# Cosine attention and GELU layer on one core: transposes earlier in the slot and in the row-sum bank, scores in twos, roots on ScalarE, preparation split over engines

## The chip, the cores and the metric

One core of a Trainium2 chip. The metric is the device time of one execution in microseconds (us), median of several; the profile is of one execution. Engines: PE (matmul), PEld (its weight loads), ACT (ScalarE), DVE (VectorE), POOL (GpSimd), SP (DMA issue). All runs named below count as fast (none is over 1.5% above the fastest of its kernel in the same session). The kernel before scatters: its fast runs lie between 735 and 747 us.

## The reference

Batch 8, 12 heads, 448 positions, head size 64; then a layer 768 to 2048 to 768.

```python
q_n = q / (norm(q) + 1e-6);  k_n = k / (norm(k) + 1e-6)
attn = softmax(q_n @ k_n.T / tau)          # tau = 0.1
x = (attn @ v), heads merged               # 3584 x 768
out = gelu_exact(x @ w_in) @ w_out
```

## The kernel before

The work goes in "pairs" of two heads, numbered g; a batch has six. A slot is one turn of the loop in `attention`. In the traces ACT, DVE, POOL and PE's matmuls run in the order in which the program gives their instructions (from 142.61 us of the kernel before DVE runs x, nq, se, rn and the copy, from 144.87 us POOL runs qkb, v, sq and sr); data and buffers add waits (POOL's qkb for rn 282.3 us in all, PE's `st` for an earlier Exp 12.6 us). The order of the calls is therefore the schedule: run 1 exchanges two calls, and the time changes by 84 us.

```python
def prep_square(g):
    nc.gpsimd.tensor_tensor(sq, qk_t[g], qk_t[g], ALU.mult)                 # POOL
    nc.vector.tensor_reduce(nq, sq, mybir.AxisListType.X, ALU.add)          # DVE
def prep_scale(g):
    nc.gpsimd.tensor_tensor(sr, nq, half, ALU.pow)                          # POOL: root
    nc.vector.tensor_scalar(se, sr, 1e-6, None, ALU.add)
    nc.vector.reciprocal(rn, se)
    for i in range(2):                                                      # q, then k
        nc.gpsimd.tensor_tensor(qkb[:, i]..., t[:, i], rn[:, i]..., ALU.mult)
def transposes(g):                       # 8 PE transposes into a bank of ps_mm
    ...
    nc.vector.tensor_copy(qkT, tp)
def scores(g, c):                        # chunk c: two matmuls, then Exp
    ...
def values(g, part):                     # part 0: o = pt*v, part 1: sm = pt*ones (row sums)
    ...
def normalise(g):
    nc.scalar.activation(ln, sm[:, :S], AF.Ln)
    nc.scalar.activation(rs, ln, AF.Exp, scale=-1.0)
    nc.vector.tensor_tensor(x_t[b][:, p, :], o[:, :S], rs, ALU.mult)

def attention(b, fill, first):           # fill: matmuls of the second dense layer ("fillers")
    for i in range(HP):
        ...
        scores(g, 0); run(u); scores(g, 1); run(u)
        if i > 0: values(g - 1, 0)
        scores(g, 2); run(u)
        if i > 0: values(g - 1, 1)
        scores(g, 3)
        if i > 0: normalise(g - 1)
        upkeep(g)                        # loads, prep_square(g+4), prep_scale(g+3)
        run(u)
        if i < HP - 1: transposes(g + 1)
        run(...)
```

After a batch's attention follows its first dense layer (16 groups of six matmuls and a Gelu). Its second layer is cut into single matmuls that fill PE's gaps in the next batch's attention. In the profiles `st` are the scores, `pt` their Exp, `hp` and `op` the products of the first and second dense layer; the "copy" is that of the transposed q and k (`qkT`), the "reduction" `nq`.

Of the kernel before, what the change touches and what calls it, by code (L numbers as in the profile page):

```python
# [8 lines left out]
F32 = mybir.dt.float32  # L9
BF16 = mybir.dt.bfloat16  # L10
AF = mybir.ActivationFunctionType
# [4 lines left out]
def kernel(  # L16
# [27 lines left out]

    consts = ctx.enter_context(tc.tile_pool(name="consts", bufs=1))
    wpool = ctx.enter_context(tc.tile_pool(name="wpool", bufs=1))
    qkp = ctx.enter_context(tc.tile_pool(name="qkp", bufs=4))
    sqp = ctx.enter_context(tc.tile_pool(name="sqp", bufs=2))
    vp = ctx.enter_context(tc.tile_pool(name="vp", bufs=8))
    nrm = ctx.enter_context(tc.tile_pool(name="nrm", bufs=3))  # L50
    qkbp = ctx.enter_context(tc.tile_pool(name="qkbp", bufs=3))
    qkTp = ctx.enter_context(tc.tile_pool(name="qkTp", bufs=3))
# [12 lines left out]
    make_identity(nc, ident)  # L65
    ones = consts.tile([CS, D], BF16)
    nc.vector.memset(ones, 1.0)
    half = consts.tile([CS, 2 * 2 * NC], F32)
    nc.vector.memset(half, 0.5)

    wi = wpool.tile([128, KD, d_ff], BF16, tag="wi")
    wo = wpool.tile([128, KF, d_model], BF16, tag="wo")
# [1 line left out]
    EXP_SET = "natural_log_exp_and_others"  # L74
    GELU_SET = "gelu_and_others"

    qk_t, v_t, sq_t, nq_t, qkb_t, qkT_t, pt_t, acc_t = {}, {}, {}, {}, {}, {}, {}, {}
    x_t, g_t = {}, {}


    def load_qk(g):
        b, p = divmod(g, HP)
        t = qkp.tile([CS, 2, 2, NC, D], F32, tag="qk", name=f"qk{g}")
        qk_t[g] = t
        for i, src in enumerate((q, k)):
            nc.sync.dma_start(
                out=t[:, i, :, :, :],
                in_=src[b, 2 * p:2 * p + 2].rearrange("h (p c) d -> p h (c d)", c=NC))

# [4 lines left out]
        nc.gpsimd.dma_start(  # L94
            out=t, in_=v[b, 2 * p:2 * p + 2].rearrange("h (p c) d -> p h (c d)", c=NC))

    def prep_square(g):
        sq = sqp.tile([CS, 2, 2, NC, D], F32, tag="sq", name=f"sq{g}")
        nc.gpsimd.tensor_tensor(sq, qk_t[g], qk_t[g], ALU.mult)  # L99
        nq = nrm.tile([CS, 2, 2, NC], F32, tag="nq", name=f"nq{g}")  # L100
        nc.vector.tensor_reduce(nq, sq, mybir.AxisListType.X, ALU.add)  # L101
        nq_t[g] = nq

    def prep_scale(g):
        nq = nq_t.pop(g)
        sr = nrm.tile([CS, 2, 2, NC], F32, tag="sr", name=f"sr{g}")
        nc.gpsimd.tensor_tensor(sr, nq, half, ALU.pow)  # L107
        se = nrm.tile([CS, 2, 2, NC], F32, tag="se", name=f"se{g}")
        nc.vector.tensor_scalar(se, sr, 1e-6, None, ALU.add)
        rn = nrm.tile([CS, 2, 2, NC], F32, tag="rn", name=f"rn{g}")  # L110
        nc.vector.reciprocal(rn, se)  # L111
        qkb = qkbp.tile([CS, 2, NC, 2, D], BF16, tag="qkb", name=f"qkb{g}")
        t = qk_t.pop(g)
        for i in range(2):
            nc.gpsimd.tensor_tensor(  # L115
                qkb[:, i].rearrange("p c h d -> p h c d"), t[:, i],
                rn[:, i].to_broadcast([CS, 2, NC, D]), ALU.mult)
        qkb_t[g] = qkb

    def transposes(g):  # L120
        qkb = qkb_t.pop(g)
        tp = ps_mm.tile([128, 2, NC, CS], BF16, tag="mm", name=f"tp{g}")
        for i in range(2):
            for c in range(NC):
                nc.tensor.transpose(tp[:, i, c, :], qkb[:, i, c].rearrange("p h d -> p (h d)"), ident)  # L125
        qkT = qkTp.tile([128, 2, NC, CS], BF16, tag="qkT", name=f"qkT{g}")
        nc.vector.tensor_copy(qkT, tp)  # L127
        qkT_t[g] = qkT


    def scores(g, c):
        qkT = qkT_t[g]
        st = ps_st.tile([CS, 2, 512], F32, tag="st", name=f"st{g}_{c}")
        for h in range(2):
            rows = slice(h * D, (h + 1) * D)
            nc.tensor.matmul(st[:, h, :S], lhsT=qkT[rows, 1, c, :], rhs=qkT[rows, 0, :, :],  # L136
                             start=True, stop=True)
        pt = ptp.tile([CS, 2, S], BF16, tag="pt", name=f"pt{g}_{c}")
        nc.scalar.activation(pt, st[:, :, :S], AF.Exp, scale=inv_tau)  # L139
        pt_t[g, c] = pt  # L140

    def values(g, part):
        if part == 0:
            acc_t[g] = (ps_acc.tile([128, 512], F32, tag="o", name=f"o{g}"),
                        ps_acc.tile([128, 512], F32, tag="sm", name=f"sm{g}"))
        dst = acc_t[g][part]
        for c in range(NC):
            for h in range(2):
                nc.tensor.matmul(dst[h * D:(h + 1) * D, :S],  # L149
                                 lhsT=v_t[g][:, h, c, :] if part == 0 else ones,  # L150
                                 rhs=pt_t[g, c][:, h, :], start=(c == 0), stop=(c == NC - 1))

    def normalise(g):
        b, p = divmod(g, HP)
        o, sm = acc_t.pop(g)
        ln = rcp.tile([128, S], F32, tag="ln", name=f"ln{g}")
        nc.scalar.activation(ln, sm[:, :S], AF.Ln)  # L157
        rs = rcp.tile([128, S], F32, tag="rs", name=f"rs{g}")
        nc.scalar.activation(rs, ln, AF.Exp, scale=-1.0)  # L159
        nc.vector.tensor_tensor(x_t[b][:, p, :], o[:, :S], rs, ALU.mult)  # L160
        v_t.pop(g)
        for c in range(NC):
            pt_t.pop((g, c))
# [29 lines left out]
    def load_wi(kd):  # L193
        nc.gpsimd.dma_start(out=wi[:, kd, :], in_=moe_w_in[kd * 128:(kd + 1) * 128, :])

    def load_wo(i):
        n = KF // 4
        nc.gpsimd.dma_start(
            out=wo[:, i * n:(i + 1) * n, :],
            in_=moe_w_out[i * n * 128:(i + 1) * n * 128, :].rearrange("(f p) d -> p f d", p=128))  # L200


    def attention(b, fill, first):
        fill = list(fill)
        per_slot = -(-len(fill) // HP)

        def run(n):
            for _ in range(min(n, len(fill))):
                fill.pop(0)()

        x_t[b] = xp.tile([128, HP, S], BF16, tag="x", name=f"x{b}")
        for i in range(HP):
            g = b * HP + i
            last_len = len(fill)
            u = per_slot // 5
            if not (i == 0 and not first):
                scores(g, 0)
                run(u)
                scores(g, 1)
            run(u)  # L220
            if i > 0:
                values(g - 1, 0)
            scores(g, 2)
            run(u)
            if i > 0:
                values(g - 1, 1)
            scores(g, 3)
            if i > 0:
                normalise(g - 1)
            upkeep(g)  # L230
            run(u)
            if i < HP - 1:
                transposes(g + 1)
            run(per_slot - (last_len - len(fill)) - (4 if len(fill) > 8 else 0))
        g = b * HP + HP - 1
        run(len(fill) - 20)
        values(g, 0)
        values(g, 1)
        normalise(g)
        run(len(fill))  # L240

    loaded = {"qk": 0, "v": 0, "sq": 0, "sc": 0}

    def upto(what, n, f):
        while loaded[what] < min(n, NG):
            f(loaded[what])
            loaded[what] += 1

    def upkeep(g):
        upto("qk", g + 6, load_qk)  # L250
        upto("v", g + 7, load_v)
        upto("sq", g + 5, prep_square)
        upto("sc", g + 4, prep_scale)


    nc.scalar.preload_act_table_set(EXP_SET)
    upto("qk", 4, load_qk)
    upto("v", 6, load_v)
    for n in range(1, 4):
        upto("sq", n, prep_square)  # L260
        upto("sc", n - 1, prep_scale)
    for kd in range(KD):
        load_wi(kd)
    for i in range(4):
        load_wo(i)
    upto("sc", 3, prep_scale)
    transposes(0)

    fill = []
    for b in range(B):  # L270
        attention(b, fill, b == 0)
        fill = []

        sb, hf = divmod(b, 2)
        if hf == 0:
            g_t[sb] = gp.tile([128, KF, 2 * S], BF16, tag="g", name=f"g{sb}")
        nc.scalar.preload_act_table_set(GELU_SET)
        for m in range(KF):
            hp = ps_mm.tile([128, 512], F32, tag="mm", name=f"hp{b}_{m}")
            for kd in range(KD):  # L280
                nc.tensor.matmul(hp[:, :S], lhsT=wi[:, kd, m * 128:(m + 1) * 128],  # L281
                                 rhs=x_t[b][:, kd, :], start=(kd == 0), stop=(kd == KD - 1))
            nc.scalar.activation(g_t[sb][:, m, hf * S:(hf + 1) * S], hp[:, :S], AF.Gelu)  # L283
            if m == KF - 3 and b + 1 < B:
                transposes((b + 1) * HP)
        if b + 1 < B:
            nc.scalar.preload_act_table_set(EXP_SET)  # L287
            scores((b + 1) * HP, 0)
            scores((b + 1) * HP, 1)
        for t in (range(3) if hf == 0 else range(3, 7)):  # L290
            fill += second_pieces(sb, t)
    for f in fill:
        f()

# [34 lines left out]
```

## Time and profile before

| | before |
|---|---|
| time, median of 4 fast runs | 744.1 us (736.4 to 745.0) |
| span of the profiled run | 734.4 us |
| busy: PE, ACT, POOL, DVE | 74%, 43%, 50%, 21% |
| first scores start | 37.1 us |
| first dense layer (batch 0) | 97.3 to 117.4 us |
| from there to the end of the last first layer, 7 periods | 591.5 us, 84.5 a period |
| rest | 25.5 us |
| granted PE clock | 0.904 |

The start until 117.4 us, the 7 periods and the rest add up to the span. No engine's share says what bounds the kernel.

### The profile page before, as it was taken

What the parts mean: (1) busy time and instruction counts of PE and PEld (TensorE: products, weight loads), DVE (VectorE), ACT (ScalarE), POOL (GpSimd) and SP (SyncE); (2) the same over time, 40 slices, a digit from 0 to 9 for tenths busy, and PEclk for the clock granted to TensorE, in tenths of its full rate; (3) what the DMA queues carried; (4) which work ended last, traced back from release to release, by engine and by line L of the source; (5) the groups of instructions that cost most, each with busy time, mean ns of one, the idle gap of its engine ahead of it and who ended that gap; (6) DMA issues with size and microseconds to landing.
All of it is one profiled execution on the core that took longest, in us unless ns stands there. A gap on an engine that the chain in (4) does not pass through costs nothing.

```text
span 734.4 us, 7898 instructions
## 1 busy us (share of the span) xinstructions
PE 545.8 (74%) x3200; PEld 249.3 (34%) x3200; DVE 156.3 (21%) x298; ACT 312.9 (43%) x432; POOL 367.2 (50%) x256
## 2 busy tenths in 40 slices
PE   0056588577968698757986879776987679867997
PEld 0022244223533244322542335322443235422454
DVE  1022211313121321231113231213212321121101
ACT  0044455444453345444453444543454444545430
POOL 8797754576256573466444762476644653330000
PEclk9999899879997999878998899887998889988999
DMA  7796210312202250032302323040502321000102
GB/s 156 153 222 126 62 33 7 78 38 54 77 12 54 79 122 17 14 97 59 79 8 54 84 55 77 6 110 8 130 7 54 82 55 48 0 23 1 43 4 84
DMA packets 42053, 45.35 MB, mean 62 GB/s; under 512 B 3360, under 2 KB 37664, under 8 KB 42016
## 3 DMA queue, kind: packets, MB, share of 16 engines
q1 hardware_dynamic: 27520, 33.04, 15.8%
q0 software_dynamic: 14496, 11.80, 10.8%
q8 instruction: 25, 0.41, 0.2%
q14 instruction: 12, 0.10, 0.0%
HBM read 45.61 MB, written 11.01 MB: 77 GB/s over the span
## 4 chain that ended last, share of the span: by engine, by line
PE 66%; DVE 12%; ACT 10%; issue 5%; POOL 4%; DMA 2%; SPq 0%; POOLq 0%
PE op L175 21%; PE hp L281 20%; PE st L136 10%; PE o L149 8%; PE sm L149 6%; DVE nq L101 4%; DVE x L160 3%; ACT rs L159 3%; ACT ln L157 3%; DVE qkT L127 3%; POOL sr L107 2%; ACT pt L139 1%; ACT L287 1%; DMA wi<-in_moe_w_in_dram 1%; ACT g L283 1%
## 5 line engine op out<-in xcount | busy, mean ns | idle before, releaser
L139 ACT ACTIVATE pt<-st 112x896 bf16<-112x896 f32 x192 | 173.4, 917 | 282.5 <-PE st L136 282.3
L115 POOL TENSOR_TENSOR qkb<-qk,rn 112x512 bf16<-112x512 f32 x96 | 98.1, 1043 | 284.5 <-DVE rn L111 282.3
L175 PE MATMUL op<-wo,g 128*128 128x384 bf16 x896 | 206.4, 365 | 0.2
L136 PE MATMUL st<-qkT 64*112 64x448 bf16 x384 | 88.8, 471 | 140.9 <-DVE qkT L127 128.1
L281 PE MATMUL hp<-x,wi 128*128 128x448 bf16 x768 | 148.1, 353 | 2.3 <-ACT g L283 1.7
L107 POOL TENSOR_TENSOR sr<-nq,half 112x16 f32<-112x16 f32 x48 | 140.2, 2920 | 0.0
L283 ACT ACTIVATE g<-hp 128x448 bf16<-128x448 f32 x128 | 69.7, 544 | 90.5 <-PE hp L281 90.5
L175 PEld LDWEIGHTS <-g 128*128 128x128 bf16 x896 | 78.3, 104 | 86.2 <-issue 56.9
L136 PEld LDWEIGHTS <-qkT 64*112 64x112 bf16 x384 | 27.3, 140 | 214.5 <-DVE qkT L127 140.3
L281 PEld LDWEIGHTS <-wi 128*128 128x128 bf16 x768 | 75.1, 98 | 72.4 <-issue 4.2
L99 POOL TENSOR_TENSOR sq<-qk 112x1024 f32<-112x1024 f32 x48 | 91.4, 1905 | 2.2 <-DMA qk<-in_k_dram 1.1
L160 DVE TENSOR_TENSOR x<-o,rs 128x448 bf16<-128x448 f32 x48 | 30.0, 625 | 243.8 <-ACT rs L159 243.8
L149 PE MATMUL o<-pt,v 112*64 112x448 bf16 x384 | 61.2, 454 | 13.5 <-DVE x L160 13.5
L127 DVE COPY qkT<-tp 128x896 bf16<-128x896 bf16 x48 | 28.3, 589 | 157.6 <-PE tp L125 157.6
L101 DVE TENSOR_REDUCE nq<-sq 112x16 f32<-112x1024 f32 x48 | 58.1, 1210 | 17.3 <-POOL sq L99 17.3
L179 DVE COPY ot<-op 128x384 f32<-128x384 f32 x56 | 30.7, 549 | 132.9 <-PE op L175 132.8
L125 PE MATMUL tp<-ident,qkb 112*128 112x112 bf16 x384 | 31.5, 234 | 27.1 <-POOL qkb L115 15.5
L149 PE MATMUL sm<-pt,ones 112*64 112x448 bf16 x384 | 49.4, 381 | 0.0
L149 PEld LDWEIGHTS <-v 112*64 112x64 bf16 x384 | 22.8, 131 | 48.5 <-issue 44.6
L125 PEld LDWEIGHTS <-qkb 112*128 112x128 bf16 x384 | 26.8, 109 | 36.2 <-POOL qkb L115 15.7
L94 POOL DMA_DIRECT2D v<-in_v_dram x48 | 35.6, 742 | 0.2 <-issue 0.2
L157 ACT ACTIVATE ln<-sm 128x448 f32<-128x448 f32 x48 | 25.8, 538 | 21.0 <-PE sm L149 21.0
(17 smaller groups left out, 96.1 us busy)
## 6 DMA issues: line engine op xcount, KB each, us to landing
qk<-in_q_dram SPq DMA_DIRECT2D x48, 224.0 KB, 4.0
qk<-in_k_dram SPq DMA_DIRECT2D x48, 224.0 KB, 4.4
v<-in_v_dram POOLq DMA_DIRECT2D x48, 112.0 KB, 3.1
wi<-in_moe_w_in_dram POOLq DMA_DIRECT2D x6, 512.0 KB, 11.1
wo<-in_moe_w_out_dram POOLq DMA_DIRECT2D x4, 768.0 KB, 24.9
out_dram<-ot SPq DMA_DIRECT2D x8, 336.0 KB, 3.1
out_dram<-ot SPq DMA_DIRECT2D x8, 288.0 KB, 3.0
out_dram<-ot SPq DMA_DIRECT2D x8, 240.0 KB, 2.9
```

What stands on the lines that cost most here:

```text
L99: nc.gpsimd.tensor_tensor(sq, qk_t[g], qk_t[g], ALU.mult)
L101: nc.vector.tensor_reduce(nq, sq, mybir.AxisListType.X, ALU.add)
L107: nc.gpsimd.tensor_tensor(sr, nq, half, ALU.pow)
L115: nc.gpsimd.tensor_tensor(qkb[:, i].rearrange("p c h d -> p h c d"), t[:, i], rn[:, i].to_broadcast([CS, 2, NC, D]), ALU.mult)
L125: nc.tensor.transpose(tp[:, i, c, :], qkb[:, i, c].rearrange("p h d -> p (h d)"), ident)
L136: nc.tensor.matmul(st[:, h, :S], lhsT=qkT[rows, 1, c, :], rhs=qkT[rows, 0, :, :], start=True, stop=True)
L139: nc.scalar.activation(pt, st[:, :, :S], AF.Exp, scale=inv_tau)
L149: nc.tensor.matmul(dst[h * D:(h + 1) * D, :S], lhsT=v_t[g][:, h, c, :] if part == 0 else ones, rhs=pt_t[g, c][:, h, :], start=(c == 0), st ...
L160: nc.vector.tensor_tensor(x_t[b][:, p, :], o[:, :S], rs, ALU.mult)
L175: nc.tensor.matmul(ps[:, :NH], lhsT=g_t[sb][:, kf, t * 128:(t + 1) * 128], rhs=wo[:, kf, ni * NH:(ni + 1) * NH], start=(kf == 0), stop=(kf ...
L281: nc.tensor.matmul(hp[:, :S], lhsT=wi[:, kd, m * 128:(m + 1) * 128], rhs=x_t[b][:, kd, :], start=(kd == 0), stop=(kd == KD - 1))
L283: nc.scalar.activation(g_t[sb][:, m, hf * S:(hf + 1) * S], hp[:, :S], AF.Gelu)
```

## The change

Its intent: keep PE from waiting at the turn of a slot, take work off POOL, and start sooner. The diff, cut to its core (buffer counts and the first pair's special cases left out):

```diff
-        nc.gpsimd.tensor_tensor(sr, nq, half, ALU.pow)
+    def root(g):
+        nc.scalar.activation(ln, nq, AF.Ln, bias=tiny)
+        nc.scalar.activation(sr, ln, AF.Exp, scale=0.5)
 ...
-        for i in range(2):
-            nc.gpsimd.tensor_tensor(
+        for i, eng in enumerate((nc.gpsimd, nc.vector)):
+            eng.tensor_tensor(
                 qkb[:, i]..., t[:, i], rn[:, i]..., ALU.mult)
 ...
-        tp = ps_mm.tile([128, 2, NC, CS], BF16, tag="mm", name=f"tp{g}")
+        tp = ps_acc.tile([128, 2, NC, CS], BF16, tag="sm", name=f"tp{g}")
 ...
+            upto("red", g + 3 if g else 2, reduce)
+            if g == 0 or i > 0:
+                scores(g, 0)                      # chunks 0 and 1
+            if i > 0:
+                run(share // 3)
+                upto("root", g + 3, root)
+                values(g - 1)                     # row sums first, then values
+                normalise(g - 1)
 ...
+            scores(g, 2)                          # chunks 2 and 3
+            if i < HP - 1:
+                transposes(g + 1)
 ...
+            upto("sc", g + 3, scale)
+            upto("sq", g + 4, square)
+            upto("qk", g + 8, load_qk)
+            upto("v", g + 4, load_v)
+            for _ in range(2 if b == 0 and i < 4 else 1):
+                if weights:
+                    weights.pop(0)()              # weight loads, one or two a slot
+            run(share - share // 3 if i else 6)
```

`upto(what, n, f)` calls `f` for every pair below n that has not had it: slot g takes the roots of pair g+2 and scales it, and squares pair g+3. `run(n)` gives n fillers. Besides, the first pair's preparation is spread over ACT, DVE and POOL, and the first two groups of a dense layer are interleaved.

More of the change, by code (lines that the diff above doesn't have):

```diff
@@ L46 @@
     wpool = ctx.enter_context(tc.tile_pool(name="wpool", bufs=1))
-    qkp = ctx.enter_context(tc.tile_pool(name="qkp", bufs=4))
+    qkp = ctx.enter_context(tc.tile_pool(name="qkp", bufs=5))
     sqp = ctx.enter_context(tc.tile_pool(name="sqp", bufs=2))
-    vp = ctx.enter_context(tc.tile_pool(name="vp", bufs=8))
+    vp = ctx.enter_context(tc.tile_pool(name="vp", bufs=6))
     nrm = ctx.enter_context(tc.tile_pool(name="nrm", bufs=3))
@@ L67 @@
     nc.vector.memset(ones, 1.0)
-    half = consts.tile([CS, 2 * 2 * NC], F32)
-    nc.vector.memset(half, 0.5)
+    tiny = consts.tile([CS, 1], F32)
+    nc.vector.memset(tiny, 1e-30)
     wi = wpool.tile([128, KD, d_ff], BF16, tag="wi")
@@ L75 @@
     GELU_SET = "gelu_and_others"
-    qk_t, v_t, sq_t, nq_t, qkb_t, qkT_t, pt_t, acc_t = {}, {}, {}, {}, {}, {}, {}, {}
+    qk_t, v_t, sq_t, nq_t, sr_t, qkb_t, qkT_t, pt_t, acc_t = {}, {}, {}, {}, {}, {}, {}, {}, {}
     x_t, g_t = {}, {}
@@ L85, in load_qk @@
         for i, src in enumerate((q, k)):
-            nc.sync.dma_start(
+            eng = nc.scalar if g == 0 and i == 1 else nc.sync
+            eng.dma_start(
                 out=t[:, i, :, :, :],
@@ L95, in load_v, with square, reduce, scale @@
             out=t, in_=v[b, 2 * p:2 * p + 2].rearrange("h (p c) d -> p h (c d)", c=NC))
-    def prep_square(g):
+    def square(g):
         sq = sqp.tile([CS, 2, 2, NC, D], F32, tag="sq", name=f"sq{g}")
-        nc.gpsimd.tensor_tensor(sq, qk_t[g], qk_t[g], ALU.mult)
-        nq = nrm.tile([CS, 2, 2, NC], F32, tag="nq", name=f"nq{g}")
-        nc.vector.tensor_reduce(nq, sq, mybir.AxisListType.X, ALU.add)
+        sq_t[g] = sq
+        t = qk_t[g]
+        if g == 0:
+            nc.scalar.activation(sq[:, 1], t[:, 1], AF.Square)
+            nc.vector.tensor_tensor(sq[:, 0], t[:, 0], t[:, 0], ALU.mult)
+        else:
+            nc.gpsimd.tensor_tensor(sq, t, t, ALU.mult)
+    def reduce(g):
+        sq = sq_t.pop(g)
+        nq = nrm.tile([CS, 2, 2, NC], F32, tag="nq", name=f"nq{g}")
+        if g == 0:
+            for i in range(2):
+                nc.vector.tensor_reduce(nq[:, i], sq[:, i], mybir.AxisListType.X, ALU.add)
+        else:
+            nc.vector.tensor_reduce(nq, sq, mybir.AxisListType.X, ALU.add)
         nq_t[g] = nq
-    def prep_scale(g):
+    def root(g):
         nq = nq_t.pop(g)
+        ln = nrm.tile([CS, 2, 2, NC], F32, tag="lq", name=f"lq{g}")
+        nc.scalar.activation(ln, nq, AF.Ln, bias=tiny)
         sr = nrm.tile([CS, 2, 2, NC], F32, tag="sr", name=f"sr{g}")
-        nc.gpsimd.tensor_tensor(sr, nq, half, ALU.pow)
+        nc.scalar.activation(sr, ln, AF.Exp, scale=0.5)
+        sr_t[g] = sr
+    def scale(g):
+        sr = sr_t.pop(g)
         se = nrm.tile([CS, 2, 2, NC], F32, tag="se", name=f"se{g}")
@@ L121, in transposes @@
         qkb = qkb_t.pop(g)
-        tp = ps_mm.tile([128, 2, NC, CS], BF16, tag="mm", name=f"tp{g}")
-        for i in range(2):
+        tp = ps_acc.tile([128, 2, NC, CS], BF16, tag="sm", name=f"tp{g}")
+        qkT = qkTp.tile([128, 2, NC, CS], BF16, tag="qkT", name=f"qkT{g}")
+        for i in (1, 0):
             for c in range(NC):
                 nc.tensor.transpose(tp[:, i, c, :], qkb[:, i, c].rearrange("p h d -> p (h d)"), ident)
-        qkT = qkTp.tile([128, 2, NC, CS], BF16, tag="qkT", name=f"qkT{g}")
@@ L127, in transposes, with scores @@
         nc.vector.tensor_copy(qkT, tp)
         qkT_t[g] = qkT
-    def scores(g, c):
+    def scores(g, c0):
         qkT = qkT_t[g]
-        st = ps_st.tile([CS, 2, 512], F32, tag="st", name=f"st{g}_{c}")
-        for h in range(2):
-            rows = slice(h * D, (h + 1) * D)
-            nc.tensor.matmul(st[:, h, :S], lhsT=qkT[rows, 1, c, :], rhs=qkT[rows, 0, :, :],
-                             start=True, stop=True)
-        pt = ptp.tile([CS, 2, S], BF16, tag="pt", name=f"pt{g}_{c}")
-        nc.scalar.activation(pt, st[:, :, :S], AF.Exp, scale=inv_tau)
-        pt_t[g, c] = pt
@@ L142, in values @@
-    def values(g, part):
-        if part == 0:
-            acc_t[g] = (ps_acc.tile([128, 512], F32, tag="o", name=f"o{g}"),
-                        ps_acc.tile([128, 512], F32, tag="sm", name=f"sm{g}"))
-        dst = acc_t[g][part]
-        for c in range(NC):
-            for h in range(2):
-                nc.tensor.matmul(dst[h * D:(h + 1) * D, :S],
-                                 lhsT=v_t[g][:, h, c, :] if part == 0 else ones,
-                                 rhs=pt_t[g, c][:, h, :], start=(c == 0), stop=(c == NC - 1))
+        for c in (c0, c0 + 1):
+            st = ps_st.tile([CS, 2, 512], F32, tag="st", name=f"st{g}_{c}")
+            for h in range(2):
+                rows = slice(h * D, (h + 1) * D)
+                nc.tensor.matmul(st[:, h, :S], lhsT=qkT[rows, 1, c, :], rhs=qkT[rows, 0, :, :],
+                                 start=True, stop=True)
+            pt = ptp.tile([CS, 2, S], BF16, tag="pt", name=f"pt{g}_{c}")
+            nc.scalar.activation(pt, st[:, :, :S], AF.Exp, scale=inv_tau)
+            pt_t[g, c] = pt
@@ new lines, in values @@
+    def values(g):
+        o = ps_acc.tile([128, 512], F32, tag="o", name=f"o{g}")
+        sm = ps_acc.tile([128, 512], F32, tag="sm", name=f"sm{g}")
+        acc_t[g] = (o, sm)
+        for dst in (sm, o):
+            for c in range(NC):
+                for h in range(2):
+                    nc.tensor.matmul(dst[h * D:(h + 1) * D, :S],
+                                     lhsT=ones if dst is sm else v_t[g][:, h, c, :],
+                                     rhs=pt_t[g, c][:, h, :], start=(c == 0), stop=(c == NC - 1))
@@ L200, in load_wo, with upto, attention @@
             in_=moe_w_out[i * n * 128:(i + 1) * n * 128, :].rearrange("(f p) d -> p f d", p=128))
-    def attention(b, fill, first):
+    weights = [lambda kd=kd: load_wi(kd) for kd in range(KD)] + [lambda i=i: load_wo(i) for i in range(4)]
+    done = {"qk": 0, "v": 0, "sq": 0, "red": 0, "root": 0, "sc": 0}
+    def upto(what, n, f):
+        while done[what] < min(n, NG):
+            f(done[what])
+            done[what] += 1
+    def attention(b, fill):
         fill = list(fill)
-        per_slot = -(-len(fill) // HP)
@@ L207, in run @@
         def run(n):
-            for _ in range(min(n, len(fill))):
+            for _ in range(max(0, min(n, len(fill)))):
                 fill.pop(0)()
         x_t[b] = xp.tile([128, HP, S], BF16, tag="x", name=f"x{b}")
+        tail = 20 if fill else 0
         for i in range(HP):
             g = b * HP + i
-            last_len = len(fill)
-            u = per_slot // 5
-            if not (i == 0 and not first):
+            share = (len(fill) - tail) // (HP - i) if i else 30
+            upto("red", g + 3 if g else 2, reduce)
+            if g == 0 or i > 0:
@@ L217, in attention @@
                 scores(g, 0)
-                run(u)
-                scores(g, 1)
-            run(u)
             if i > 0:
-                values(g - 1, 0)
-            scores(g, 2)
-            run(u)
-            if i > 0:
-                values(g - 1, 1)
-            scores(g, 3)
-            if i > 0:
-                normalise(g - 1)
-            upkeep(g)
-            run(u)
+                run(share // 3)
+                upto("root", g + 3, root)
+                values(g - 1)
+                normalise(g - 1)
+            else:
+                run(24)
+                upto("root", g + 3 if g else 2, root)
@@ L232, in attention @@
+            if g == 0:
+                upto("sc", 2, scale)
+            scores(g, 2)
             if i < HP - 1:
                 transposes(g + 1)
-            run(per_slot - (last_len - len(fill)) - (4 if len(fill) > 8 else 0))
+            if g == 0:
+                upto("sq", 3, square)
+                upto("red", 3, reduce)
+                upto("root", 3, root)
+            upto("sc", g + 3, scale)
+            upto("sq", g + 4, square)
+            upto("qk", g + 8, load_qk)
+            upto("v", g + 4, load_v)
@@ L235, in attention @@
+            for _ in range(2 if b == 0 and i < 4 else 1):
+                if weights:
+                    weights.pop(0)()
+            run(share - share // 3 if i else 6)
         g = b * HP + HP - 1
-        run(len(fill) - 20)
-        values(g, 0)
-        values(g, 1)
+        run(len(fill) - 8)
+        values(g)
         normalise(g)
         run(len(fill))
-    loaded = {"qk": 0, "v": 0, "sq": 0, "sc": 0}
-    def upto(what, n, f):
-        while loaded[what] < min(n, NG):
-            f(loaded[what])
-            loaded[what] += 1
@@ L249, in upkeep @@
-    def upkeep(g):
-        upto("qk", g + 6, load_qk)
-        upto("v", g + 7, load_v)
-        upto("sq", g + 5, prep_square)
-        upto("sc", g + 4, prep_scale)
-    nc.scalar.preload_act_table_set(EXP_SET)
-    upto("qk", 4, load_qk)
-    upto("v", 6, load_v)
-    for n in range(1, 4):
-        upto("sq", n, prep_square)
-        upto("sc", n - 1, prep_scale)
-    for kd in range(KD):
-        load_wi(kd)
-    for i in range(4):
-        load_wo(i)
-    upto("sc", 3, prep_scale)
-    transposes(0)
@@ L269, with first @@
-    fill = []
-    for b in range(B):
-        attention(b, fill, b == 0)
-        fill = []
+    def first(b):
         sb, hf = divmod(b, 2)
@@ L277, with mm, gelu @@
         nc.scalar.preload_act_table_set(GELU_SET)
-        for m in range(KF):
-            hp = ps_mm.tile([128, 512], F32, tag="mm", name=f"hp{b}_{m}")
-            for kd in range(KD):
-                nc.tensor.matmul(hp[:, :S], lhsT=wi[:, kd, m * 128:(m + 1) * 128],
-                                 rhs=x_t[b][:, kd, :], start=(kd == 0), stop=(kd == KD - 1))
-            nc.scalar.activation(g_t[sb][:, m, hf * S:(hf + 1) * S], hp[:, :S], AF.Gelu)
-            if m == KF - 3 and b + 1 < B:
-                transposes((b + 1) * HP)
+        hps = {}
+        def mm(m, kds):
+            for kd in kds:
+                nc.tensor.matmul(hps[m][:, :S], lhsT=wi[:, kd, m * 128:(m + 1) * 128],
+                                 rhs=x_t[b][:, kd, :], start=(kd == 0), stop=(kd == KD - 1))
+        def gelu(m):
+            nc.scalar.activation(g_t[sb][:, m, hf * S:(hf + 1) * S], hps.pop(m)[:, :S], AF.Gelu)
+        for m in range(KF):
+            if m == KF - 5 and b + 1 < B:
+                transposes((b + 1) * HP)
+            if m != 1:
+                hps[m] = ps_mm.tile([128, 512], F32, tag="mm", name=f"hp{b}_{m}")
+            if m == 0:
+                hps[1] = ps_mm.tile([128, 512], F32, tag="mm", name=f"hp{b}_1")
+                mm(0, range(KD - 1))
+                mm(1, range(KD - 1))
+                mm(0, (KD - 1,))
+            else:
+                mm(m, (KD - 1,) if m == 1 else range(KD))
+            gelu(m)
         if b + 1 < B:
@@ L288 @@
             scores((b + 1) * HP, 0)
-            scores((b + 1) * HP, 1)
-        for t in (range(3) if hf == 0 else range(3, 7)):
-            fill += second_pieces(sb, t)
+    upto("qk", 1, load_qk)
+    nc.scalar.preload_act_table_set(EXP_SET)
+    upto("qk", 5, load_qk)
+    upto("v", 3, load_v)
+    upto("sq", 1, square)
+    upto("red", 1, reduce)
+    upto("sq", 2, square)
+    upto("root", 1, root)
+    upto("sc", 1, scale)
+    transposes(0)
+    fill = []
+    for b in range(B):
+        attention(b, fill)
+        first(b)
+        sb, hf = divmod(b, 2)
+        fill = [f for t in (range(3) if hf == 0 else range(3, 7)) for f in second_pieces(sb, t)]
     for f in fill:
```

## The prediction

The ring's sum came to 8.05 us: the steps that stand add up to 6.98, and two terms are cut, one for the root's two instructions (with it the sum was 7.5) and one for a longer time of POOL's half beside DVE's. Both are also in H+11.9, in the four rounds of 32.2 us, in the 26.8, 59 and 63.8 us of the start and in the totals 68.3, 69, 82 and 590.5.

The 0.7 us for cold stretches is derived from no trace. "Cold" is a low granted PE clock, such as the 0.56 at 145.2 to 148.4 us of the kernel before and the 0.50 at 156.8 to 160 us; "warm" is 1.00.

> **What bounds the kernel now.** I first read the busy table by stage, because a share over the whole span mixes an attention stage with a dense matmul stage. The columns are the stretch, its length, busy time of PE, PEld, DVE, ACT and POOL, the granted PE clock, DMA share and GB/s.
>
> ```profile
> 37.00:99.25 62.25, 36.28 (x190) 14.49 (x190) 16.37 (x31) 28.03 (x37) 49.96 (x35) 0.92 0.59 121
> 118.00:183.20 65.20, 46.73 (x277) 19.62 (x276) 16.18 (x31) 30.43 (x38) 40.00 (x29) 0.84 0.22 50
> 183.20:202.80 19.60, 19.36 (x110) 9.93 (x108) 2.64 (x5) 8.72 (x17) 5.08 (x3) 1.00 0.29 74
> ```
>
> Attention of one batch takes 65.2 us (even batches 66.6), the first dense layer 19.6 us. In the dense layer PE is busy throughout at clock 1.00; the change cannot shorten that. In attention no engine fills the stretch: PE 46.7 of 65.2 at a clock of only 0.84, ACT 30, POOL 40. So it is bound by a chain of waits. The chain that ended last, read over one slot (a head pair) of that stretch, shows which:
>
> ```profile
> 141.43 0.55 ACT ln L157
> ...
> 142.00 0.58 ACT rs L159
> ...
> 142.61 0.62 DVE x L160
> 143.24 1.12 DVE nq L101
> ...
> 144.73 0.49 DVE qkT L127
> ...
> 145.26 0.40 PE st L136 x2
> ...
> 151.77 0.79 issue
> ```
>
> The same ln comes again at 152.56: the slot is 11.1 us. Up to 145.26 PE stands (scores of the next pair need qkT, and its copy stands on DVE behind x and the reduction nq). Then PE works through scores, fillers (L175), values and row sums until 151.73; the 0.79 us is the rest of the last Exp; then ln, rs, x again. So about 4.3 us of PE idle a slot are in the loop, and the 6.5 us of PE work are slow besides: by stretches, the clock was 0.56 at 145.2 to 148.4 and 0.92 at 148.4 to 152.5. POOL is not in this loop, although it is the busiest after PE there:
>
> ```profile
> L107 POOL TENSOR_TENSOR sr<-nq,half 112x16 f32<-112x16 f32 x48 | 140.2, 2920 | 0.0
> ...
> L99 POOL TENSOR_TENSOR sq<-qk 112x1024 f32<-112x1024 f32 x48 | 91.4, 1905 | 2.2 <-DMA qk<-in_k_dram 1.1
> ```
>
> The third thing is the start, read in the timeline:
>
> ```profile
> 23.26 3.32 POOL L194 DMA_DIRECT2D wi<-in_moe_w_in_dram  x6
> ...
> 33.16 2.93 POOL L107 TENSOR_TENSOR sr<-nq,half 112x16 f32<-112x16 f32 x1
> ...
> 37.11 0.99 PE L136 MATMUL st<-qkT 64*112 64x448 bf16 x4 [20.51 <-DVE qkT L127]
> ```
>
> The first scores wait until 37.1 us although the transposes of pair 0 were done at 16.6: the copy stands on DVE behind the scaling of pair 2, whose root stood on POOL behind ten weight issues, two of which waited 3.6 us for earlier weights to land.
>
> [...]
>
> **The change part by part.**
> Removed: 48 POOL roots of 2.92 us (140 us busy), and one of the two POOL scalings of a pair (1.04). POOL busy time falls from 7.7 us a pair (2.92 + 2×1.04 + 1.91 + 0.74, the last for issuing v) to 1.04+1.91+0.74 = 3.7. None of that was in the slot's loop, only in the start. [...]
>
> PE order: fillers, row sums, values, scores of chunks 2 and 3, then the transposes of the next pair in the row-sum bank, then more fillers. Scores of the next pair no longer wait for ln, rs, x and nq in a row. Work per slot at the warm rates of the chain: scores 0.8, sums 0.88, values 0.88, transposes 0.56, fillers 0.165 each; 9 fillers in odd batches (96, less 30 in slot 0 and 20 at the end, over 5) make 4.6 us, 15.6 in even ones 5.7. [...] If nothing else waited a slot would take 5.5 to 6 us.
>
> But the order of the built program makes a new loop, through POOL. Root(g+3) on ACT stands ahead of ln(g). It needs the reduction of sq(g+3); sq(g+3) stands on POOL behind the Q scaling of pair g+2; that needs rn(g+2), which on DVE stands behind x(g-1) and the copy qkT(g+1); and x needs ln(g-1), which stands on ACT behind root(g+2). Once round is one slot:
> [...] ln 0.57; rs 0.61; x 0.54; copy 0.48; se 0.20; rn until POOL starts 0.39; Q scaling 0.99; sq 1.95; reduction 1.25. The durations are start-to-start steps of the trace before[...]. Sum 7.5 us. The K half reaches DVE about 0.1 us before the Q half reaches POOL (0.14 us from rn's end to POOL's start in the trace)[...].
> PE then idles (8.05 less 4.6 to 5.7) 2.4 to 3.4 us a slot[...].
>
> A batch, from the end H of the dense layer before: the last Gelu, a table load of 1.28 and two Exp go beside 24 fillers (4 us); scores, transposes and copy until H+6.0; then se, rn, POOL, reduction, root: H+11.9. Four rounds: +32.2. Then ln and rs 1.2, two Exp 1.75, sums and values 1.85, eight fillers 1.3: 50.1 us. Dense layer 18.2. In all 68.3 us where the kernel before needs 85.3 (84.5 and 86.2 alternating). For cold stretches I add 0.7: 69.
>
> Start: pair 1 lands at 8.5 us, as now; POOL squares it (1.9), scales Q of pair 0 (1.0); transposes, copy, first scores at 12.6 us instead of 37.1. Pairs 1 and 2 ramp up one after the other (root, scaling, square, reduction each), root(3) about 26.8, four rounds to 59, then 2.95 and 1.85 to 63.8, dense layer to 82; before it ended at 117.4. Weights: the software queue's 10.8% of the span are 79 us of all 16 DMA engines for 11.8 MB, so 6.3 MB of weights need 42 us, spread over slots 0 to 5; with 13 pairs of q, k (1.6 us each) and 10 of v (0.8) about 71 us, just in time for the second layer at 82.
> End: 25.5 us from the last dense layer's end, unchanged.
> Sum: 82 + 7×69 + 25.5 = 590.5 us span. Timed runs before lie between 736.4 and 744 for a span of 734.4, so I add little: 592.
>
> **Rivals.**
> (a) The loop through POOL is looser than I think, and PE and ACT bound the slot at about 6 us: 36 to 40 rounds less 2 us, about 515. For it: POOL is busy only 3.7 us a slot. Against: the order of the instructions, which is fixed.
> [...]
> (c) PE drops to half clock in every slot and becomes the bound with 15.6 fillers[...]: slots of 8.5 to 9.5, about 625.
> (d) The weights, now spread, land late or hold POOL's queue in the first batch: 5 to 15 us more. For it: weight pieces took 11 to 25 us to land. Against: the sum above.
>
> **Range and chances.** The stretches that the change touches lose 35 us at the start and 7×16.3 later; even rival (c) with (d) stays near 640. Rounds of 7 to 9 us give 550 to 634; I take 545 to 632. Faster by over 2% is as good as certain (98 in 100); the rest is for a fault I overlooked.
>
> **What would show it right or wrong.** Right: in the chain, slots of about 8 us in which Q scaling, sq (POOL), nq (DVE), Ln, Exp, ln, rs (ACT), x and the copy follow each other, with PE hardly in it outside the dense layer; the same slot in odd and even batches; POOL idle only ahead of qkb, put down to rn; one of POOL's qkb and DVE's new one longer than alone, or started late; first scores near 12.6 us. Wrong: slots near 6 us with PE on the chain (a), slots that grow with the fillers and a clock below 0.7 (c), waits of hp or op for DMA (d), a first dense layer that ends far from 82.

## The result, and the profile after

| | before | after | predicted |
|---|---|---|---|
| time, median of 4 fast runs | 744.1 us | 584.2 us (583.9 to 585.6) | 592 (545 to 632) |
| span of the profiled run | 734.4 | 582.6 | 590.5 |
| first scores start | 37.1 | 11.6 | 12.6 |
| end of first dense layer | 117.4 | 82.8 | 82 |
| seven periods | 591.5 | 474.3 | 483 |
| rest | 25.5 | 25.5 | 25.5 |
| POOL busy | 367 | 196 | |
| PE busy, clock | 546, 0.904 | 492, 0.945 | |

The ratio is 0.787 (95% interval 0.782 to 0.793). Ratios are the mean time of one kernel's fast runs over that of the other's in the same rounds, so not quite the ratio of the medians. The profiled execution of the kernel before took 736.2 us, less than the median; so the spans differ by less than the medians do. All outputs are right.

Of the span's 151.8 us, 34.6 came from the start and 117.2 from the seven periods. The busy table by stage (stretch, length, busy time and count of PE, PEld, DVE, ACT, POOL, clock, DMA share, GB/s) for the kernel after, attention of batch 1 and its dense layer:

```profile
83.30:131.60 48.30, 38.75 (x277) 19.13 (x278) 21.19 (x39) 31.63 (x51) 22.63 (x17) 0.93 0.33 78
131.60:150.80 19.20, 18.76 (x107) 9.69 (x106) 2.31 (x3) 8.38 (x17) 0.97 (x2) 1.00 0.19 47
```

Attention went from 65.2 to 48.3 us; still no engine fills it, and POOL is now busy for less than half of it, where it was busy for 40 of 65 us. The shares of the chain that ended last, by engine, for the kernel after:

```profile
PE 49%; POOL 20%; DVE 16%; ACT 9%; issue 4%; DMA 1%; POOLq 0%; SPq 0%
```

POOL was 4% of the chain at 367 us of work and is 20% at 196. The chain over one slot (start, length, what) shows how:

```profile
105.37 1.45 POOL qkb L135
106.82 1.86 POOL sq L106
...
108.70 1.23 DVE nq L115
...
109.96 0.32 ACT lq L121
...
110.30 0.22 ACT sr L123
110.51 0.44 ACT ln L178
...
111.00 0.57 PE tp L146 x8
...
111.59 0.63 DVE x L181
112.21 0.53 DVE qkT L147
...
113.29 1.45 POOL qkb L135
```

This is the ring that the prediction wrote down: Q scaling, square, reduction, root, normalising, copy, and the next Q scaling 7.92 us later. PE is in it with the eight transposes only, which wait for ln, because they write the bank that it reads, and end at the same moment as rs (111.6 us). The rounds repeat at 7.9 us in odd and even batches alike. The two halves of the scaling, in the groups of the kernel after (busy time, mean ns of one, idle time before them):

```profile
L135 POOL TENSOR_TENSOR qkb<-qk,rn 112x512 bf16<-112x512 f32 x48 | 70.3, 1464 | 324.4 <-DVE rn L131 284.7
...
L135 DVE TENSOR_TENSOR qkb<-qk,rn 112x512 bf16<-112x512 f32 x48 | 34.1, 710 | 1.8 <-DVE rn L131 0.2
```

POOL's half has the same shape as before, when it took 1043 ns. Now it takes 1464.

### The profile page after: what moved, and what is told of

Same layout as the page of the kernel before. It is cut to its first block, busy times and chain, and to the rows that moved or that the text cites. A ratio compares the mean times of both kernels' runs of the same rounds, so it can differ in the third digit from the quotient of the medians.

```text
span 582.6 us, 7930 instructions
## 1 busy us (share of the span) xinstructions
PE 492.1 (84%) x3200; PEld 248.1 (43%) x3200; DVE 195.6 (34%) x348; ACT 324.7 (56%) x529; POOL 196.3 (34%) x159
## 4 chain that ended last, share of the span: by engine, by line
PE 49%; POOL 20%; DVE 16%; ACT 9%; issue 4%; DMA 1%; POOLq 0%; SPq 0%
PE hp L289 25%; PE op L196 15%; POOL sq L106 12%; POOL qkb L135 9%; DVE nq L115 7%; DVE qkT L147 3%; DVE x L181 3%; PE tp L146 3%; ACT ln L178 3%; PE st L157 2%; ACT lq L121 2%; PE o L170 2%; ACT rs L180 2%; PE sm L170 2%; DVE rn L131 2%
## 5 line engine op out<-in xcount | busy, mean ns | idle before, releaser
L160 ACT ACTIVATE pt<-st 112x896 bf16<-112x896 f32 x192 | 164.9, 910 | 34.0 <-PE st L157 33.4
L135 POOL TENSOR_TENSOR qkb<-qk,rn 112x512 bf16<-112x512 f32 x48 | 70.3, 1464 | 324.4 <-DVE rn L131 284.7
L196 PE MATMUL op<-wo,g 128*128 128x384 bf16 x896 | 175.6, 346 | 0.0
L196 PEld LDWEIGHTS <-g 128*128 128x128 bf16 x896 | 85.2, 102 | 70.8 <-issue 28.2
L146 PE MATMUL tp<-ident,qkb 112*128 112x112 bf16 x384 | 30.1, 226 | 69.3 <-ACT ln L178 58.2
L157 PE MATMUL st<-qkT 64*112 64x448 bf16 x384 | 65.7, 413 | 9.1 <-DVE qkT L147 8.0
L121 ACT ACTIVATE lq<-nq,tiny 112x16 f32<-112x16 f32 x48 | 14.8, 308 | 96.8 <-DVE nq L115 95.7
L170 PE MATMUL o<-pt,v 112*64 112x448 bf16 x384 | 48.7, 379 | 0.0
L157 PEld LDWEIGHTS <-qkT 64*112 64x112 bf16 x384 | 22.2, 136 | 49.9 <-issue 28.0
L135 DVE TENSOR_TENSOR qkb<-qk,rn 112x512 bf16<-112x512 f32 x48 | 34.1, 710 | 1.8 <-DVE rn L131 0.2
L170 PEld LDWEIGHTS <-ones 112*64 112x64 bf16 x384 | 19.8, 118 | 32.8 <-issue 27.0
```

What stands on the lines that cost most here:

```text
L135: eng.tensor_tensor(qkb[:, i].rearrange("p c h d -> p h c d"), t[:, i], rn[:, i].to_broadcast([CS, 2, NC, D]), ALU.mult)
L146: nc.tensor.transpose(tp[:, i, c, :], qkb[:, i, c].rearrange("p h d -> p (h d)"), ident)
L157: nc.tensor.matmul(st[:, h, :S], lhsT=qkT[rows, 1, c, :], rhs=qkT[rows, 0, :, :], start=True, stop=True)
L160: nc.scalar.activation(pt, st[:, :, :S], AF.Exp, scale=inv_tau)
L170: nc.tensor.matmul(dst[h * D:(h + 1) * D, :S], lhsT=ones if dst is sm else v_t[g][:, h, c, :], rhs=pt_t[g, c][:, h, :], start=(c == 0), st ...
L196: nc.tensor.matmul(ps[:, :NH], lhsT=g_t[sb][:, kf, t * 128:(t + 1) * 128], rhs=wo[:, kf, ni * NH:(ni + 1) * NH], start=(kf == 0), stop=(kf ...
```

## The experiments

The theory to be tested: the kernel after is bound by the ring of 7.92 us, not by any engine's work; the kernel before by ln, rs, x, nq and the copy in a row ahead of the next scores. The main rival: PE, cold in places (clock 0.60 from 113.3 to 116.3 us of the kernel after) and 84% busy, sets the time, and the gain came from work taken off POOL.

**1. The square first.** Only the order of two calls:

```diff
-            upto("sc", g + 3, scale)
-            upto("sq", g + 4, square)
+            upto("sq", g + 4, square)
+            upto("sc", g + 3, scale)
```

> Edit: in the changed kernel the square of pair g+3 is given to POOL ahead of the scaling of pair g+2, nothing else. Theory (the slot of 7.92 us is the ring root, ln, rs, x, copy, se, rn, Q scaling, square, reduction, root; the square is in it only because it stands behind the Q scaling on POOL): the square is done in POOL's idle time, the ring is cut at rn, and a slot falls to what comes next, about 5.9 us (ACT 5.1, PE 4.6 to 5.7, and a shorter ring through the K half and the reduction on DVE, about 5.2). Five rounds a batch less 2 us: about 500 us, 485 to 520. Rival (PE, cold between bursts, sets the slot, and POOL's place on the chain is only an effect): within 2% of 584.

Measured: 499.9 us (497.9 to 500.7), 0.678 of the kernel before. The slots are 5.0 to 5.5 us in odd batches and 5.1 to 5.9 in even ones, which have more fillers; PE is 94% busy at a clock of 0.995, and the chain by engine reads:

```profile
PE 78%; DVE 10%; ACT 7%; issue 2%; DMA 1%; POOL 1%; SPq 0%; POOLq 0%
```

POOL fell from 20% of the chain to 1% with the same instructions. The rival falls. What bounds this kernel is, by its chain, PE for the most part, and in the first slots of odd batches the shorter ring through the K half (5.05 us a round).

**2. The K half later.** The scaling is cut into two calls; DVE's comes after the next reduction:

```diff
             upto("red", g + 3 if g else 2, reduce)
+            if g:
+                upto("sk", g + 2, scale_k)       # K half, on DVE
 ...
-            upto("qk", g + 8, load_qk)
+            upto("qk", g + 7, load_qk)
```

> Edit: the K half of the scaling on DVE is given one slot later, after the next reduction, so that it no longer runs beside POOL's Q half (q and k are loaded one pair less ahead, so that their buffers suffice). Theory ([...] POOL's Q half takes 1.46 us instead of 1.04 because of that): POOL's qkb has a mean of 1.02 to 1.06 us, the slot falls from 7.92 to about 7.45 us, 38 rounds: 567 us, 560 to 575. Rival (POOL's qkb is longer for another reason, or the wait moves to the transposes): qkb stays above 1.3 us or the time within 5 us of 584.

Measured: 567.6 us (566.6 to 568.0). POOL's half in the groups of this run:

```profile
L138 POOL TENSOR_TENSOR qkb<-qk,rn 112x512 bf16<-112x512 f32 x48 | 50.9, 1060 | 327.6 <-DVE rn L131 232.2 <-PE st L164 46.4 <-DMA out_dram<-ot 25.9
```

Apart from DVE's half it takes 1060 ns again, and the Q scalings follow each other at 7.48 us. So the overlap with DVE costs POOL 0.4 us a pair, and 17 us in all.

**3 and 4. The same additional work on POOL, inside and outside the ring.** One more multiplication of a pair, result unused, at one of two places:

```diff
             upto("sc", g + 3, scale)
+            if done["sq"] < min(g + 4, NG):      # run 3: between scaling and square
+                more(done["sq"])
             upto("sq", g + 4, square)
             ...
             upto("v", g + 4, load_v)
+            if g + 3 < NG:                       # run 4: after the square and the v issue
+                more(g + 3)
```

> Edit: one more multiplication of POOL of 1.9 us a pair, its result unused, put between the Q scaling and the square, in the ring. Theory: each of some 38 rounds is 1.87 us longer: 584 + 71 = 655 us, 645 to 665; slots of 9.8 us. Rival (POOL has 4 us of idle time a slot and is not the bound): under 595.

> Edit: the same additional multiplication of 1.9 us a pair, put behind the square and the v issue, where POOL waits for the next rn. Theory: POOL's busy time grows by the same 90 us as in the run before, but outside the ring: within 6 us of 584, slots stay at 7.9 us. Rival (the sum of POOL's work counts[...]): 600 to 655.

Measured: 653.5 us (652.5 to 660.9) inside, 584.5 us (583.8 to 585.6) outside. POOL's busy time is the same in both (280 and 282 us, against 196). Inside, the rounds are 9.78 us; outside, 7.92. POOL's busy time bounds nothing; its place in the order does.

**5. The root by POOL's power again,** in the place in which Ln and Exp stood:

```diff
-        nc.scalar.activation(ln, nq, AF.Ln, bias=tiny)
-        nc.scalar.activation(sr, ln, AF.Exp, scale=0.5)
+        nc.gpsimd.tensor_tensor(sr, nq, half, ALU.pow)
```

> Edit: in the changed kernel the root is again POOL's power of 2.92 us, in the place in which the Ln and Exp stood; all else as changed. Theory: the ring loses root, ln, rs, x and copy (ln no longer stands behind the root) and becomes power 2.92, se and rn 0.7, Q scaling 1.45, square 1.86, reduction 1.25: 8.15 us instead of 7.92, so 38 rounds are 9 us, with 3 at the start: 596 us, 588 to 606. Rival (taking 140 us of power off POOL is a main part of the gain): 2.4 us a round more, 660 to 680.

Measured: 592.3 us (592.0 to 593.2). The sum was right, its division was not. The rounds are 8.24 us, as worked out, but the seven periods together are as long as in the kernel after: what the longer rounds cost comes back elsewhere in each batch. The last ln of a batch no longer stands behind a root and may start sooner; that this is the reason is argued from the order, not shown. Of the 8.6 us of span, 8.4 lie ahead of the end of the first dense layer (91.1 us instead of 82.8). So the roots on ScalarE, which take 140 us of work off POOL, are worth 8 us here, all at the start.

**6. The kernel before with its transposes early,** nothing else:

```diff
             if i > 0:
                 values(g - 1, 1)
+            if i < HP - 1:
+                transposes(g + 1)
             scores(g, 3)
             if i > 0:
                 normalise(g - 1)
             upkeep(g)
             run(u)
-            if i < HP - 1:
-                transposes(g + 1)
```

> Edit: in the kernel before, only the transposes and the copy of the next pair are given ahead of the last scores, the normalising and the preparation; all else as before. Theory (the kernel before is bound by ln, rs, x, nq and the copy standing in a row on DVE ahead of the next scores): that ring falls away and POOL's row of v issue, square, power, two scalings takes its place, about 8.3 us a slot instead of 11.1 to 12: 16 us a batch, about 625 us, 600 to 650. Rival (the gain of the change needs the other parts: roots off POOL, chunks in twos, the bank): above 700 us.

Measured: 611.1 us (609.3 to 613.9), 0.821 of the kernel before; faster than the 625 I expected. The chain of this run, one round:

```profile
126.23 0.69 POOL v L94
...
126.95 1.90 POOL sq L99
128.85 2.88 POOL sr L107
...
133.37 1.04 POOL qkb L115
134.41 0.69 POOL v L94
```

POOL's row is 8.18 us a slot. The stages settle what the other parts of the change are worth: this run's first dense layer ends at 108.9 us, its seven periods take 474.7 us, the rest 25.6. The kernel after: 82.8, 474.3, 25.5. So this one move gives as much as the whole change does in the seven periods, and 8.5 us of the start; the other 26 us of the change lie at the start. Two things to keep in mind: the move is not quite that of the change, where the transposes stand behind the normalising, though ahead of the preparation and the last fillers; and the two kernels agree over the seven periods although they follow different rings (8.18 and 7.92 us).

**7. The transposes back in the dense layers' banks.**

```diff
-        tp = ps_acc.tile([128, 2, NC, CS], BF16, tag="sm", name=f"tp{g}")
+        tp = ps_mm.tile([128, 2, NC, CS], BF16, tag="mm", name=f"tp{g}")
```

> Edit: in the changed kernel the transposes again use the bank pair of the dense layers' products instead of the row-sum bank. Theory (the transposes' wait for ln is beside the ring: x comes later in any case): 584 us within 6. Rival (the bank matters): over 10 us slower for waits on fillers' copies, or over 10 us faster because the wait for ln is gone.

Measured: 587.9 us (586.1 to 588.1): within what was expected. The wait of the transposes for ln, 58.2 us in the list of waits of the kernel after, cost nothing.

**8. The weights up front.** All ten weight loads are issued right after pair 0 is prepared.

```diff
     transposes(0)
+    for f in weights:
+        f()
+    weights.clear()
```

> Edit: all ten weight loads are again issued by POOL in a row, right after pair 0 is prepared, instead of one or two a slot. Theory (with the roots off POOL the weight issues only hold up the scaling of pair 1 by their 6.4 us of issue and a few us of waiting, and crowd the loads): first scores still near 11.6 us, all later things 5 to 10 us later: 590 us, 586 to 596. Rival (the spreading of the weights is most of the 35 us gained at the start): 605 to 620.

Measured: 590.5 us (588.1 to 591.9). First scores at 11.4 us; POOL's half of pair 1 at 20.8 instead of 15.0 us, after two waits of 2.2 us for earlier weights. The first dense layer ends 5.4 us later. Spreading the weights is about a sixth of what the start gained.

**9. Both orders together:** the edits of runs 1 and 2.

> Edit: the square first and the K half one slot later, both together. Theory (with the square first PE is 94% busy at clock 0.995 and sets most of the slot; only the first slots of a batch still follow a ring through the K half and the reduction): 0 to 5 us less than the 499.9 of square first alone: 494 to 501. Rival (the two gains of 84 and 17 us add): 483.

Measured: 495.1 us (494.9 to 497.6), 0.670 of the kernel before (0.666 to 0.674): the fastest version found, by 1% (the ratio of run 1 was 0.673 to 0.683). What it gains on run 1 lies in the first batch, whose dense layer ends at 66.6 instead of 69.7 us; the seven periods take 401.2 and 400.9. The gains of 84 and 17 us do not add: PE is 94% busy in both, and there is little waiting left to remove.

**10. The additional POOL work with the ring cut.** The multiplication of run 3 ahead of the square of run 1:

```diff
-            upto("sc", g + 3, scale)
+            if done["sq"] < min(g + 4, NG):
+                more(done["sq"])
             upto("sq", g + 4, square)
+            upto("sc", g + 3, scale)
```

> Edit: the square first, and the additional POOL multiplication of 1.9 us a pair ahead of it, so again ahead of the next scaling. Theory (the ring is cut; POOL now only needs its own work done in a slot: 1.46 + 1.89 + 1.89 + 0.71 = 5.95 us against slots of 5.0 to 5.5): about half a microsecond a slot, 515 to 530 us. Rival (POOL work ahead of the scaling costs its full length here too): 500 + 71 = 571 us.

Measured: 526.1 us (525.8 to 526.8), so 26 us for 1.9 us a pair, not 69 as in the ring. The slots are 6.37 us, where I had 5.95. The difference is not POOL's sum: DVE's small addition se takes 1.30 us in the mean of this run, 0.19 in the kernel after and 0.23 in run 1. With one more instruction ahead of it, POOL's square now runs when the addition comes. Of its 39 long additions 38 end within 0.05 us of the end of the square beside them, so they wait for POOL. By the chain a round is now the short ring of run 1 with that wait in it: 6.35 us instead of 5.05, the addition 1.40 instead of 0.09. And 11 of the 26 us lie in the first batch, whose later slots take 7.4 to 7.6 us.

**11. Scores one chunk at a time** (the order of the change otherwise kept):

```diff
-                scores(g, 0)
-                run(share // 3)
+                scores(g, 0, 1)
+                run(share // 6)
+                scores(g, 1, 1)
+                run(share // 3 - share // 6)
 ...
-            scores(g, 2)
+            scores(g, 2, 1)
+            if i:
+                run(share // 6)
+            scores(g, 3, 1)
```

> Edit: in the changed kernel the scores are again given one chunk at a time, with fillers between them, instead of two. Theory (the ring through POOL has no score in it): 584 us within 6. Rival (two chunks at a time are part of the gain): over 10 us slower.

Measured: 585.4 us (583.2 to 587.1). Scores in twos are worth nothing while the ring lasts. What they would be worth with the ring cut was not tried.

**12. The square first, with the root by power:** the edits of runs 1 and 5.

> Edit: the square first, but the root by POOL's power. Theory (the root on ScalarE is worth nothing as long as the ring lasts, but once it is cut POOL's own sum counts: 2.93 + 1.46 + 1.89 + 0.71 = 7.0 us a slot against 5.3): 38 slots of 1.7 us more than 500: 560 us, 545 to 575. Rival (the root is never worth anything): 500 to 510.

Measured: 569.5 us (568.1 to 571.2). So the root on ScalarE is worth about 70 us on top of the square first (runs 12 and 1; 23 of them before the end of the first dense layer), and 8 without it. The rounds are 7.5 us, not 7.0, for the same reason as in run 10. The chain of this run:

```profile
101.62 2.94 POOL sr L121
...
104.59 1.88 DVE se L127
```

The addition of 16 elements a partition lasts as long as POOL's square, which started 0.06 us ahead of it.

## Why the prediction was right

The measured 584.2 us lies inside the range and 8 us below the middle. By its own steps:

- **What bounded the kernel before.** Right, and shown by run 6: with only the transposes moved ahead of the row ln, rs, x, nq, that row is gone, and the seven periods are as short as in the full change.
- **The new ring.** Right in its members and nearly in size: 8.05 us predicted, with the two terms that are cut above, 7.92 measured. Runs 1, 3 and 4 show it by cutting it, by lengthening it and by the same work beside it. By the same start-to-start steps (timeline, 105.35 to 113.26 us) the Q scaling beside DVE's half takes 1.44 us and the root's two 0.46, and every other step is within 0.05 of what I had.
- **The two halves side by side.** That POOL's takes longer beside DVE's was right, shown by run 2; measured were 0.42 us a pair (1464 less 1043 ns).
- **The batch.** Predicted 68.3 us plus 0.7 for cold stretches; measured 68.3 in the mean of the first six. One term of it was mis-sized: the dense layer takes 19.3 us, not 18.2. I had read 18.2 off the first batch of the kernel before, where five matmuls had run ahead of the stretch that I read; its other batches have 19.1. Attention takes 49.0 us where I had 50.1 (its terms add up to 50.2). The two errors cancel; that the sum is right to a tenth is luck. The addition for the cold clock was not needed: PE did run cold in places (clock 0.60 from 113.3 to 116.3 us), but the rounds before and after were both 7.92 us.
- **The last period** is 64.3 us, shorter than the others in every run here; that it is because nothing is left to prepare is argued from the order of the calls. I had counted it as 69. This (4.7 us) and the 0.7 of six periods (4) make the 8 us.
- **The start.** 11.6 us to the first scores and 82.8 to the end of the first dense layer, against 12.6 and 82. The slots of that batch were 5.8 to 8.0 us long. Pair 1 could be squared at 6.4 us, not at 8.5 as I had it, and the first addition waited for that square (1.31 us instead of 0.17).
- **A reading that was too long.** I wrote 4.3 us of PE idle a slot; the gaps before the scores are 3.70 and 4.16 us there, since the eight transposes run in the time that I counted. Nor did every such gap bring the clock down: after 3.83 us, at 67.2 and at 77.3 us of the kernel before, the granted clock was 1.00 over the next 5 us, though the eight matmuls of the values took 1.70 and 1.71 us there, against 0.95 at 178.2 us.
- **The rivals.** (a) slots of 6 us, against which I held the order of the instructions: run 1 reached it, at 500 us, only by changing that order. (b), that POOL's half is not longer beside DVE's: it was, 1464 ns against 1043. (c) PE cold and the bound: no. (d) weights late: the first dense layer and the fillers wait for no weight in the list of waits after.

What I did not see: that an earlier place for the transposes alone would give as much as the whole change outside the start. I set the parts out one by one but did not ask what each would bring by itself; I took POOL's work before as "not in the loop" and did not say that it would have made nearly the same loop (8.18 us) once the other was gone.

## What to carry to other kernels

When a change removes a row of waits, write down the next closed ring of instructions across the engines' orders, once round per iteration, before counting busy time: here it foretold the time to within 2%, although POOL, through which the ring runs, is busy for only a third of the span. (How near the total came is in part luck, as said; the ring itself was foretold to 0.13 us, but 1.07 of its 8.05 us were the two terms that no trace of the kernel before could show.) An instruction that an engine could do early, but that the program gives to it behind one that waits, is the first thing to move: two exchanged lines brought 84 us. And test the parts of a change alone, since what a part is worth depends on which ring is the longest (the root on ScalarE: 8 us or 70).

## What the traces show besides

- POOL's scaling starts some 0.1 us after DVE's of 0.69 us (105.35 and 105.23 us of the kernel after) and takes 1464 ns in the mean, against 1043 in the kernel before and 1060 in run 2, where DVE's half comes apart: 0.4 us lost of an overlap of some 0.6.
- In these runs a wait of DVE for POOL stands inside the busy time of the instruction that waits, not as idle time. DVE's addition on 16 elements a partition has a mean of 0.17 us in the kernel before, 1.30 in run 10 and 1.51 in run 12, when POOL's square of 1.9 us runs beside it.
- In the kernel after, a PE gap of 2.56 us (108.4 to 111.0 us) was followed by a mean granted clock of 0.78 to 113.3 us and 0.60 to 116.3 us. The length of a gap alone does not decide: after another gap of 2.56 us (254.1 to 256.7 us) the clock stayed at 1.00 over the next 5 us, as it did after the gaps of 1.5 us at 102 and 117 us.
- ScalarE's Ln and Exp of the root, on 16 elements a partition, take 308 and 216 ns; those on 448 elements 538 (ln) and 576 (rs) in the kernel before, 530 and 577 in the kernel after.
- POOL's power operation takes 2.92 us for 16 elements a partition, more than its multiplication of 1024 (1.9 us).
